# Block 0 of MLP1: tiles 4 to 15 in three passes of halves, and the three low bits of a decoded weight from ScalarE

## The chip, the cores and the metric

One core of a Trainium2 chip runs the whole program. The time is the device time of one execution in microseconds (us), the median of three runs. The profile is one further execution, with its own time. PE is TensorE's matmul stream, DVE is VectorE, ACT is ScalarE, SP is the engine that issues nearly all transfers.

## The reference, cut to what matters

```
kv  = einsum('bhsd,bhse->bhde', k, v);  out = einsum('bhsd,bhde->bhse', q, kv)   # 8 x 8 x 576 x 64
x   = out / sqrt(mean(out*out, -1) + 1e-6) * g_norm          # then as 4608 tokens x 512
h   = x @ w_in                                               # 512 -> 2048
g   = h * clip(h + 3, 0, 6) / 6
x1  = g @ w_out                                              # 2048 -> 512
out = (silu(x1 @ w_gate) * (x1 @ w_val)) @ w_out2            # 512 -> 1536 -> 512
```

`q`, `k`, `v` and `g_norm` come as 4-byte floats. The five weight matrices come as 8-byte floats, which no engine multiplies: the kernel reads each as two 4-byte words and puts a 4-byte float together from them.

## The kernel before, in words

The 4608 tokens are nine blocks of 512. Features lie on the partitions, tokens run along the free axis, so that `x` of a block is four tiles of 128x512 (`x_f[0][0..3]`), `h` is 16 tiles `h_0` to `h_15`, and `acc` four tiles in PSUM.

**Precision and what a product costs.** A plain 4-byte float product (`mm`, L116 to L118) is one MATMUL row in the program that PE works off at the float rate. The other form splits each operand into a high and a low half of the type fp32r, `split` (L106 to L109): ACT copies the tile to the high half (L108), DVE subtracts it from the tile for the low half (L109). The product is then three passes (`mm3`, L111 to L114): high times low, low times high, high times high.

**Decoding a weight.** `decode_w` (L154) makes a tile of 128x512 out of a raw tile of 128x4x128x2 words (512 KB). ACT scales the high word, read as a float (`decode_scale`, L167). Then DVE does three operations (`decode_bits`): a shift by three and a mask (L176, one tensor in and out), the sign by a bitwise or (L179), and the three low bits out of the raw tile's low word (L182). Raw tiles have three buffers, taken in turn by `raw_i` (w_in) and `raw_o` (w_out). The last reader of a raw tile is L182, and the load that takes its buffer next waits for that on SP's queue, L139 for w_in and L148 for w_out.

**Block 0** is where the weights of MLP1 are decoded. Its tiles are named by f: w_in tile f is `w_i{f}`, w_out tile f is `w_o{f}`. The loop starts behind the first stretch (whose order is written by hand, tiles 0 and 1 among it) and runs over c. In step c: `h_whole([c], 0)` makes `h_c` from `w_i{c}` with four plain products (L118); the attention for block 1 goes on, a third of a head pair per step (`kv` and `qT`, then `at` and `sq`, then `ss` and the norm L330 to L353); `o_first(c-2)` adds `g_{c-2}` times w_out to the four `acc` tiles in 12 passes (L112 to L114) and writes the halves of `w_o` to memory (`wod`); `get_o(c+1)` and `get_i(c+4)` decode and, for w_out, split (`wh_o`, `wl_o`); `raw_o(c+3)` and `raw_i(c+6)` load. Between `h` and `g` stand ACT's relu (L426), DVE's product (L427) and a split.

The four `split_x(1, ...)` and `split_wi` at the loop's end make the halves of block 1's x and of w_in tiles 0 to 3. From block 1 on, everything is made of halves: `split_wi` of tiles 4 to 7 stands in block 1's loop, and `make_wi` combines w_in tiles in pairs. The weights of MLP2 go through the same `decode_w` (24 tiles of gate and value, 12 of w_out2), most of them while the blocks of MLP1 and the first steps of MLP2 run.

**What sets the order.** PE's order is the order written in the program. In the block's loop the orders of ACT, DVE and SP come from the scheduler, which lays each engine's operations out by its own times; each engine then works its list off strictly in that order. So an operation that waits holds up all behind it on its engine.

Of the kernel before, what the change touches and what calls it, by code (L numbers as in the profile page):

```python
# [8 lines left out]
F32 = mybir.dt.float32  # L9
F32R = mybir.dt.float32r  # L10
U32 = mybir.dt.uint32
AF = mybir.ActivationFunctionType
ALU = mybir.AluOpType
AX = mybir.AxisListType
# [4 lines left out]
def kernel(  # L19
# [27 lines left out]
    nc = tc.nc  # L47
    P = 128
# [5 lines left out]
    KD = DM // P  # L54
    NF = DFF // P
    NF2 = DFF2 // P
    T = 512
    TQ = T // 2
# [12 lines left out]
    TO2 = TO // 2  # L71
    NP1 = NF // 2
    PWHOLE = 4

    def block_pieces(j):

# [47 lines left out]
    shift = const.tile([P, 1], F32, name="shift")  # L124
    gn38 = const.tile([P, 1], F32, name="gn38")
    three = const.tile([P, 1], F32, name="three")

    wod = dram.tile([NF, P, 2 * DM], F32, name="wod")
    x1d = dram.tile([P, KD, NT], F32, name="x1d")
# [23 lines left out]
    def w_slot(name, dtype):  # L153
        return wpool.tile([P, KD, P], dtype, tag="w", name=name)  # L154

    def decode_w(raw, name):

        return decode_bits(raw, decode_scale(raw, name))

    def decode_scale(raw, name):

        t = w_slot(f"w_{name}", F32)
        nc.scalar.activation(  # L167
            out=t, in_=raw[:, :, :, 1].bitcast(F32), func=AF.Copy, scale=2.0 ** -112
        )
        return t  # L170

    def decode_bits(raw, t):

        lw, hw = raw[:, :, :, 0], raw[:, :, :, 1]
        u = t.bitcast(U32)
        nc.vector.tensor_scalar(  # L176
            u, u, 3, 0x7FFFFFFF, op0=ALU.logical_shift_left, op1=ALU.bitwise_and
        )
        nc.vector.scalar_tensor_tensor(  # L179
            out=u, in0=hw, scalar=0x80000000, in1=u, op0=ALU.bitwise_and, op1=ALU.bitwise_or  # L180
        )
        nc.vector.scalar_tensor_tensor(  # L182
            out=u, in0=lw, scalar=29, in1=u, op0=ALU.logical_shift_right, op1=ALU.bitwise_or
        )
        return t
# [233 lines left out]
    def h_whole(cs, j):  # L419

        pss = {}
        for kk in range(KD):
            h_part(cs, j, kk, pss)
        for f, ps in pss.items():
            t = w_slot(f"t_{j}_{f}", F32).rearrange("p k f -> p (k f)")
            nc.scalar.activation(out=t, in_=ps, func=AF.Relu, bias=three[:, 0:1])  # L426
            nc.vector.scalar_tensor_tensor(  # L427
                out=t, in0=t, scalar=6.0, in1=ps, op0=ALU.min, op1=ALU.mult
            )
            split_g(j, f, t)  # L430

    whl, xhl = {}, {}

    def split_wi(f):
        whl[f] = split_w(wi[f], f"s{f}")

    def split_x(j, kk):

        if kk < 3:
            t = xpool.tile([P, 2, 2, TQ], F32R, tag=("B11", "B22", "B21")[kk], name=f"xs_{j}_{kk}")  # L440
            hi, lo = (t[:, i].rearrange("p k c -> p (k c)") for i in range(2))
        else:
            hi, lo = (w_slot(f"xs{o}_{j}_{kk}", F32R).rearrange("p k f -> p (k f)") for o in "hl")
        split(hi, lo, x_f[j][kk])
        xhl[kk] = hi, lo

    def h_part(cs, j, kk, pss):

        for f in cs:
            if kk == 0:  # L450
                pss[f] = pmm.tile([P, 512], F32, tag="mm", name=f"h_{j}_{f}")
            st, sp = kk == 0, kk == KD - 1
            if j:
                (wh, wl), (xh, xl) = whl[f], xhl[kk]
                mm3(pss[f], wh[:, kk], wl[:, kk], xh, xl, st, sp)
            else:
                mm(pss[f], wi[f][:, kk], x_f[j][kk], st, sp)
# [86 lines left out]
    def prepare_x1(j):  # L544

        x = x_f.pop(j)
        for key in XKEYS:
            if j == 1 and key[0] == "B":
                b = ("B11", "B12", "B21", "B22").index(key)
                xo1[key] = tuple(  # L550
                    [xhl[b // 2 * 2 + kk][i][:, b % 2 * TQ:(b % 2 + 1) * TQ] for kk in range(2)]
                    for i in range(2)
                )
                continue
            t = xpool.tile([P, 2, 2, TQ], F32R, tag=key, name=f"{key}_{j}")
            xo1[key] = t[:, 0], t[:, 1]

        def part(b, kk):

            c = slice(b % 2 * TQ, (b % 2 + 1) * TQ)  # L560
            if isinstance(x, list):
                return x[b // 2 * 2 + kk][:, c]
            return x[:, b // 2 * 2:b // 2 * 2 + 2, c]

        ts = {}
        for key, a, b in (("T1", 1, 0), ("T2", 3, "T1"), ("T3", 3, 1), ("T4", "T2", 2)):
            ts[key] = fpool.tile([P, 2, TQ], F32, tag="f", name=f"{key}_{j}")
            for kk in range(2) if isinstance(x, list) else (slice(None),):
                a_, b_ = (ts[o][:, kk] if isinstance(o, str) else part(o, kk) for o in (a, b))
                nc.vector.tensor_tensor(out=ts[key][:, kk], in0=a_, in1=b_, op=ALU.subtract)  # L570
        for key, b in (
            ("B11", 0), ("T1", None), ("T2", None), ("T3", None), ("B22", 3), ("B21", 2),
            ("T4", None),
        ):
            hi, lo = xo1[key]
            if isinstance(hi, list):
                continue
            if b is None:
                split(hi, lo, ts[key])
            else:  # L580
                for kk in range(2) if isinstance(x, list) else (slice(None),):
                    split(hi[:, kk], lo[:, kk], part(b, kk))
# [307 lines left out]
    with tc.manual_schedule(engines={mybir.EngineType.PE}):  # L890
# [3 lines left out]
            mybir.EngineType.Activation, mybir.EngineType.DVE, mybir.EngineType.SP,  # L894
        }))
        nc.vector.memset(eps, EPS)
        warm = const.tile([P, 1], F32, name="warm")
        for hp in range(NP):
            load_q(0, hp)
# [238 lines left out]
        for c in range(NF + LAG):  # L1138
            if c < NF:
                if c >= GROUP:  # L1140
                    h_whole([c], 0)
                for s, a in att_actions(1, (2, 5, 8, 11)):
                    if s == c:
                        a()
            if c >= LAG:
                o_first(c - LAG)
            if c >= NF + LAG - KD:
                split_x(1, c - NF - LAG + KD)
                split_wi(c - NF - LAG + KD)
            if c < NF:  # L1150
                get_o(c + 1)
                raw_o(c + 3)
                get_i(c + 4)
                raw_i(c + 6)
# [13 lines left out]
        for j in range(1, NB):  # L1168
            pairs = list(range(NP1))
            if j == 2:  # L1170
                pairs = pairs[PWHOLE:] + pairs[:PWHOLE]
            for i, p in enumerate(pairs):
                if j == 1 and p < PWHOLE:
                    hpair_whole(j, p)
                    if p == 0:
                        prepare_x1(j)
                else:
                    hpair(j, p)
                if j == 1 and i < 2:
                    for f in (2 * i + 4, 2 * i + 5):  # L1180
                        split_wi(f)
                if j == 1 and 2 <= i < 6:
                    make_wi(i + 2)
                if j == 2 and 1 <= i < 5:
                    make_wi(i - 1)
                for f in (2 * p, 2 * p + 1):
                    load_wo(f)
                if j + 1 < NB:
                    for s, a in att_actions(j + 1, (0, 1, 3, 4)):
                        if s == i:  # L1190
                            a()
                if i:
                    o_pair(j, pairs[i - 1], i == 1, False)
                if i == NP1 - 1:
                    if 1 < j + 1 < NB:
                        prepare_x1(j + 1)
                    o_pair(j, p, False, True)
                if j == NB - 1:
                    if i == NP1 - 2:
                        parts = prepare_x(0, x1, fpool)  # L1200
                        next(parts)
                    if i == 0:
                        ph1.__exit__(None, None, None)
                        big["xr"], raw2, big["x"] = (
                            mlp2.enter_context(tc.tile_pool(name=o, bufs=1, side="right"))
                            for o in ("xr", "raw2", "x1")
                        )
                        x1 = big["xr"].tile([P, KD, T2], F32, tag="xr", bufs=1, name="xr_0")
                    if 1 <= i <= KD:
                        nc.sync.dma_start(out=x1[:, i - 1], in_=x1d[:, i - 1, :T2])  # L1210
                    for _ in range(1 + (i % 2 and i < NP1 - 3)):
                        load_second()
            x1_out(j)
# [136 lines left out]
```

## Time and profile before

| | |
|---|---|
| three runs | 1677.17, 1678.15, 1678.41 us, median 1678.15 |
| the profiled execution | 1676.15 us, its span 1674.4 us |
| PE busy | 1655.1 us, 99% of the span |
| DVE busy | 1321.0 us, 79% |
| ACT busy | 809.4 us, 48% |
| PE's granted clock | 1.00 in each of 40 slices |

The span is the time between the first and the last event that the profile shows; 1.75 us of the execution lie around it. A busy share is a mean over stages with different limits. Block 0's loop lies between 35.59 us (the end of the first stretch) and 140.15 us (the end of `o_first(15)`). A wait is what ended the idle time of an engine.

### The profile page before, as it was taken

The page shows a single profiled execution, that of the slowest core. Times are in us where ns is not written, and L with a number is a line of the kernel's source. Part 1 is how long each engine was busy: PE and PEld are TensorE (multiplying, and loading weights), DVE is VectorE, ACT ScalarE, POOL GpSimd, SP SyncE. Part 2 cuts the span into 40 slices and gives each one's busy share as a digit, 9 for nine tenths or more (in the row PEclk, how much of TensorE's full clock was granted, in tenths as well). Part 3 has the DMA queues.
Part 4 walks back from the last instruction along what each step waited for, and adds up shares of the span by engine and source line. Part 5 has one row for each costly group of instructions (what it writes and reads, how often), then busy time and mean ns, then how long its engine had stood idle before and what let it go on. Part 6 is the DMA issues. An engine that isn't in the chain of part 4 may idle for free.

```text
span 1674.4 us, 27998 instructions
## 1 busy us (share of the span) xinstructions
PE 1655.1 (99%) x10640; PEld 1525.7 (91%) x10640; DVE 1321.0 (79%) x2535; ACT 809.4 (48%) x1489; POOL 2.4 (0%) x7
## 2 busy tenths in 40 slices
PE   7999999999999999999999999999999999999999
PEld 4567889899989899989889999999999999999999
DVE  6888997677787777677989988778998676887774
ACT  5655564544444454545565444444454444444432
POOL 0000000000000000000000000000000000000000
PEclk9999999999999999999999999999999999999999
DMA  8885445444535544325564544485453357655642
GB/s 233 260 260 177 135 146 145 146 133 146 148 113 157 142 141 130 126 98 185 170 202 166 195 161 146 175 275 191 164 190 144 138 208 272 214 194 196 217 159 97
DMA packets 224999, 288.63 MB, mean 172 GB/s; under 512 B 80992, under 2 KB 139360, under 8 KB 224864
## 3 DMA queue, kind: packets, MB, share of 16 engines
q1 hardware_dynamic: 220480, 285.80, 52.5%
q8 instruction: 83, 1.36, 0.3%
q10 hardware_dynamic: 4384, 1.05, 0.3%
q14 instruction: 52, 0.43, 0.1%
HBM read 211.03 MB, written 75.76 MB: 171 GB/s over the span
## 4 chain that ended last, share of the span: by engine, by line
PE 82%; DVE 10%; DMA 4%; ACT 3%; issue 1%; SPq 0%; DVEq 0%; ACTq 0%
PE q_g L588 15%; PE q_v L588 15%; PE a L588 7%; PE acc L112 6%; PE acc L113 6%; PE acc L114 6%; PE c L588 4%; PE o2c L836 4%; PE o2d L836 4%; PE o2a L836 4%; PE d L588 4%; PE o2e L836 2%; DVE g L109 1%; PE kv L271 1%; DMA raw_o<-in_moe_w_out_dram 1%
## 5 line engine op out<-in xcount | busy, mean ns | idle before, releaser
L112 PE MATMUL acc<-g,wo 128*128 128x512 f32 x512 | 202.3, 395 | 0.6 <-DVE g L109 0.6
L113 PE MATMUL acc<-g,wo 128*128 128x512 f32 x512 | 199.9, 390 | 0.0
L114 PE MATMUL acc<-g,wo 128*128 128x512 f32 x512 | 199.4, 390 | 0.0
L633 ACT ACTIVATE t<-h,three 128x512 f32<-128x512 f32 x120 | 86.9, 724 | 144.5 <-DVE h L630 113.1
L108 ACT ACTIVATE g<-t 128x512 fp32r<-128x512 f32 x142 | 89.5, 630 | 67.5 <-DVE t L634 55.6
L109 DVE TENSOR_TENSOR g<-t,g 128x512 fp32r<-128x512 f32 x142 | 96.6, 680 | 30.9 <-ACT g L108 30.3
L112 PEld LDWEIGHTS acc<-g,wo 128*128 128x128 f32 x512 | 96.2, 188 | 21.3 <-DVE g L109 1.5
L114 PEld LDWEIGHTS acc<-g,wo 128*128 128x128 f32 x512 | 96.1, 188 | 20.6
L113 PEld LDWEIGHTS acc<-g,wo 128*128 128x128 f32 x512 | 96.3, 188 | 18.3
L634 DVE SCALAR_TENSOR_TENSOR t<-t,h 128x512 f32<-128x512 f32 x120 | 82.4, 687 | 31.1 <-ACT t L633 29.7
L723 ACT ACTIVATE hg<-q_g 128x384 f32<-128x384 f32 x36 | 17.7, 491 | 117.5 <-PE q_g L588 117.5
L588 PE MATMUL q_v<-hT,v 128*128 128x384 f32 x288 | 73.6, 336 | 0.0
L730 DVE TENSOR_TENSOR hv<-hg,hv 128x1536 f32<-128x1536 f32 x36 | 63.1, 1753 | 5.1 <-ACT hv L723 4.9
L118 PE MATMUL h<-x,w_i 128*128 128x512 f32 x128 | 57.9, 595 | 2.3 <-DVE w_i L182 1.2
L723 ACT ACTIVATE hv<-q_v 128x384 f32<-128x384 f32 x36 | 17.7, 491 | 87.3 <-PE q_v L588 87.3
L712 DVE TENSOR_TENSOR h1v<-h1v,q_v 128x384 f32<-128x384 f32 x36 | 19.9, 553 | 48.3 <-ACT h1v L711 47.2
L588 PE MATMUL q_v<-hB,v 128*128 128x384 f32 x216 | 54.9, 335 | 0.0
L728 ACT ACTIVATE hg<-hg 128x1536 f32<-128x1536 f32 x36 | 53.6, 1490 | 0.9
L588 PE MATMUL a<-T,wh_i 128*128 128x256 f32 x240 | 53.2, 284 | 0.7 <-ACT s L607 0.5
L588 PE MATMUL c<-T,wh_i 128*128 128x256 f32 x240 | 53.0, 283 | 0.0
L588 PE MATMUL d<-T,wh_i 128*128 128x256 f32 x240 | 53.0, 283 | 0.0
L588 PEld LDWEIGHTS q_v<-hT,v 128*128 128x128 f32 x288 | 52.3, 188 | 0.0
(611 smaller groups left out, 5389.4 us busy)
## 6 DMA issues: line engine op xcount, KB each, us to landing
wo<-wod SPq DMA_DIRECT2D x128, 512.0 KB, 3.4
g2d<-hv SPq DMA_DIRECT2D x36, 768.0 KB, 3.7
graw<-g2d SPq DMA_DIRECT2D x26, 1024.0 KB, 7.2
xr<-x1d SPq DMA_DIRECT2D x10, 1536.0 KB, 7.0
gb<-g2d SPq DMA_DIRECT2D x54, 256.0 KB, 4.8
x1d<-x1o SPq DMA_DIRECT2D x36, 256.0 KB, 2.9
out_dram<-o SPq DMA_DIRECT2D x36, 256.0 KB, 2.5
raw_i<-in_moe_w_in_dram SPq DMA_DIRECT2D x16, 512.0 KB, 5.3
```

The lines of the kernel that those rows point to most:

```text
L108: nc.scalar.activation(out=hi, in_=src, func=AF.Copy)
L109: nc.vector.tensor_tensor(out=lo, in0=src, in1=f32(hi), op=ALU.subtract)
L112: nc.tensor.matmul(out_, wh, xl, start=start, stop=False)
L113: nc.tensor.matmul(out_, wl, xh, start=False, stop=False)
L114: nc.tensor.matmul(out_, wh, xh, start=False, stop=stop)
L118: nc.tensor.matmul(out_, f32(w), f32(x), start=start, stop=stop)
L588: nc.tensor.matmul(ps, a[:, kk], b[kk] if isinstance(b, list) else b[:, kk], start=first and n == 0, stop=n == 5, skip_group_check=True,)
L633: nc.scalar.activation(out=t, in_=h[i], func=AF.Relu, bias=three[:, 0:1])
L634: nc.vector.scalar_tensor_tensor(out=t, in0=t, scalar=6.0, in1=h[i], op0=ALU.min, op1=ALU.mult)
L728: nc.scalar.activation(out=hg, in_=hg, func=AF.Silu)
L730: nc.vector.tensor_tensor(out=hv, in0=hg, in1=hv, op=ALU.mult)
L836: nc.tensor.matmul(ps[:, i * TO2:(i + 1) * TO2], a[:, cs], b, start=first and i == 0 and n == 0, stop=n == 2, skip_group_check=True,)
```

## The change

Part one: block 0's tiles 4 to 15 are made of three passes of halves, as in later blocks. The halves of block 0's x (`split_x(0, kk)`, two calls each in steps 1 and 2) and of w_in tiles 4 to 15 (`split_wi(c + 2)`, one call a step) are made in the loop; those of tiles 4 to 7 are kept, so that block 1 need not make them again, those of tiles 8 to 15 are dropped. Part two: in `decode_w` ACT makes a second tile `y` out of the raw tile, the upper 16 bits of the low word times 2^-13 and less almost one half, rounded to an integer; DVE shifts the scaled tile by three and takes `y` in, in one operation (L171 of after), and then the sign (L174). The tiles of the first stretch (w_in 0 to 2, w_out 0) keep the old form.

```
-        return decode_bits(raw, decode_scale(raw, name))
+        t = decode_scale(raw, name)
+        y = w_slot(f"y_{name}", U32)
+        nc.scalar.activation(
+            out=y, in_=top16(raw), func=AF.Identity, scale=2.0 ** -13, bias=half[:, 0:1]
+        )
+        u = t.bitcast(U32)
+        nc.vector.scalar_tensor_tensor(
+            out=u, in0=u, scalar=3, in1=y, op0=ALU.logical_shift_left, op1=ALU.bitwise_or
+        )
+        nc.vector.scalar_tensor_tensor(
+            out=u, in0=raw[:, :, :, 1], scalar=0x80000000, in1=u,
+            op0=ALU.bitwise_and, op1=ALU.bitwise_or,
+        )
+        return t
+
+    def top16(raw):
+        r = raw.rearrange("p k f t -> p (k f t)").bitcast(U16)
+        return r.rearrange("p (k f t) -> p k f t", k=KD, t=4)[:, :, :, 1]
...
     def split_x(j, kk):
-        if kk < 3:
+        if j and kk < 3:
...
-            if j:
-                (wh, wl), (xh, xl) = whl[f], xhl[kk]
+            if j or f >= FWHOLE:
+                (wh, wl), (xh, xl) = whl[f], xhl[j, kk]
                 mm3(pss[f], wh[:, kk], wl[:, kk], xh, xl, st, sp)
             else:
                 mm(pss[f], wi[f][:, kk], x_f[j][kk], st, sp)
...
                 if c >= GROUP:
                     h_whole([c], 0)
+                    if c >= 2 * PWHOLE:
+                        whl.pop(c)
...
+            if 1 <= c <= 2:
+                for kk in (2 * c - 2, 2 * c - 1):
+                    split_x(0, kk)
+            if FWHOLE <= c + 2 < NF:
+                split_wi(c + 2)
...
-                if j == 1 and i < 2:
-                    for f in (2 * i + 4, 2 * i + 5):
-                        split_wi(f)
```

DVE, before, ahead of tile 4 and for the tiles around it: `w_i5` and `w_o3` are decoded, `t_0_2` and `g_0_2` are the gate of tile 2, `wl_o2` and `wl_o3` low halves of w_out.

```order
L109 TENSOR_TENSOR wl_o2_456<-w_o2_450,wh_o2_455 128x512
L176 TENSOR_SCALAR w_i5_461<-w_i5_461 128x512
L179 SCALAR_TENSOR_TENSOR w_i5_461<-raw_i5_423,w_i5_461 128x512
L427 SCALAR_TENSOR_TENSOR t_0_2_473<-t_0_2_473,h_0_2_468 128x512
L182 SCALAR_TENSOR_TENSOR w_i5_461<-raw_i5_423,w_i5_461 128x512
L176 TENSOR_SCALAR w_o3_536<-w_o3_536 128x512
L109 TENSOR_TENSOR g_0_2_476<-t_0_2_473,g_0_2_476 128x512
```

The same place on DVE, after: `wl_s4` is the low half of w_in tile 4, which `h_4` now needs, and `xsl_0_2` and `xsl_0_3` are low halves of block 0's x (those of 0 and 1 stand a few rows ahead).

```order
L111 TENSOR_TENSOR wl_o2_470<-w_o2_463,wh_o2_469 128x512
L171 SCALAR_TENSOR_TENSOR w_i5_475<-w_i5_475,y_i5_477 128x512
L448 SCALAR_TENSOR_TENSOR t_0_2_488<-t_0_2_488,h_0_2_483 128x512
L174 SCALAR_TENSOR_TENSOR w_i5_475<-raw_i5_425,w_i5_475 128x512
L111 TENSOR_TENSOR xsl_0_2_552<-x_0_2_347,xsh_0_2_551 128x512
L111 TENSOR_TENSOR g_0_2_491<-t_0_2_488,g_0_2_491 128x512
L111 TENSOR_TENSOR xsl_0_3_556<-x_0_3_349,xsh_0_3_555 128x512
L111 TENSOR_TENSOR wl_s4_560<-w_i4_447,wh_s4_559 128x512
L171 SCALAR_TENSOR_TENSOR w_o3_563<-w_o3_563,y_o3_565 128x512
```

What `h_4` waits for on DVE has moved from the decode of `w_i4`, ahead of these rows, to the eighth of them.

ACT, before, one step in the middle of the loop, from the split of `w_o6` to that of `w_o7` (`rs` and `nw` belong to the norm of block 1).

```order
L108 ACTIVATE wh_o6_729<-w_o6_724 128x512
L167 ACTIVATE w_i9_735<-raw_i9_604 128x512
L426 ACTIVATE t_0_6_747<-h_0_6_742,three_94 128x512
L167 ACTIVATE w_o7_776<-raw_o7_651 128x512
L108 ACTIVATE g_0_6_750<-t_0_6_747 128x512
L330 ACTIVATE rs_807<-ss_1_1_805,eps_91 128x512
L339 ACTIVATE nw_808<-rs_807 128x512
L344 ACTIVATE nw_808<-nw_808,shift_92 128x512
L108 ACTIVATE wh_o7_781<-w_o7_776 128x512
```

The same step on ACT, after.

```order
L110 ACTIVATE wh_o6_791<-w_o6_785 128x512
L188 ACTIVATE w_i9_797<-raw_i9_639 128x512
L167 ACTIVATE y_i9_799<-raw_i9_639,half_95 128x512
L447 ACTIVATE t_0_6_818<-h_0_6_805,three_94 128x512
L110 ACTIVATE wh_s8_847<-w_i8_701 128x512
L351 ACTIVATE rs_892<-ss_1_1_890,eps_91 128x512
L110 ACTIVATE g_0_6_821<-t_0_6_818 128x512
L188 ACTIVATE w_o7_851<-raw_o7_699 128x512
L167 ACTIVATE y_o7_853<-raw_o7_699,half_95 128x512
L360 ACTIVATE nw_893<-rs_892 128x512
L365 ACTIVATE nw_893<-nw_893,shift_92 128x512
L110 ACTIVATE wh_o7_857<-w_o7_851 128x512
```

Three operations have come in (`y_i9`, `wh_s8`, `y_o7`), and the scale of `w_o7` has moved behind `g_0_6`. PE's rows stay where they were; each of the tiles 4 to 15 has 12 rows for 4.

## Rows read from the trace of the kernel before

**Rows 1.** Windows (stretch, length, then busy time of each engine, granted clock, DMA).
```profile
35.59:64.25 28.66, 26.24 (x129) 16.82 (x129) 26.22 (x55) 17.11 (x35) 0.00 (x0) 1.00 0.73 225
64.25:85.93 21.68, 21.68 (x94) 13.56 (x93) 19.75 (x37) 13.19 (x24) 0.00 (x0) 1.00 0.87 284
...
800.00:1000.00 200.00, 198.17 (x1138) 188.73 (x1137) 180.00 (x345) 106.96 (x196) 0.00 (x0) 1.00 0.52 179
```
**Rows 2.** What PE waited for, 35.59 to 140.15 (total us, times, longest).
```profile
PE qT L289 <- DMA wod<-wl_o: 1.1, 1, 1.1
PE h L118 <- DVE t L427: 0.8, 1, 0.8
PE h L118 <- DVE w_i L182: 0.5, 1, 0.5
PE acc L112 <- DVE g L109: 0.3, 1, 0.3
```
**Rows 3.** PE's timeline (start, duration, group, in brackets the idle time before).
```profile
44.73 0.40 PE L112 MATMUL acc<-g,wh_o 128*128 128x512 f32 x1
...
47.47 3.60 PE L118 MATMUL h<-x,w_i 128*128 128x512 f32 x8
50.90 1.02 PE L118 MATMUL ss<-sq,ones 128*128 128x512 f32 x2
...
137.29 0.50 PE L112 MATMUL acc<-g,wh_o 128*128 128x512 f32 x1 [0.30 <-DVE g L109]
```
**Rows 4.** What ACT waited for most, 35.59 to 140.15.
```profile
ACT wh_o L108 <- DVE w_o L182: 19.0, 12, 2.8
```
**Rows 5.** DVE's timeline about tile 4, and the last gate.
```profile
44.57 0.69 DVE L182 SCALAR_TENSOR_TENSOR w_i<-raw_i,w_i 128x512 uint32<-128x512 uint32 x1
...
46.56 0.69 DVE L109 TENSOR_TENSOR wl_o<-w_o,wh_o 128x512 fp32r<-128x512 f32 x1 [0.70 <-ACT wh_o L108]
47.16 0.42 DVE L176 TENSOR_SCALAR w_i<-w_i 128x512 uint32<-128x512 uint32 x1
47.62 0.69 DVE L179 SCALAR_TENSOR_TENSOR w_i<-raw_i,w_i 128x512 uint32<-128x512 uint32 x1
48.34 0.69 DVE L427 SCALAR_TENSOR_TENSOR t<-t,h 128x512 f32<-128x512 f32 x1
...
136.55 0.68 DVE L109 TENSOR_TENSOR g<-t,g 128x512 fp32r<-128x512 f32 x1
```
**Rows 6.** ACT's timeline in the middle of the loop, and the last `wh_o`.
```profile
65.39 0.63 ACT L108 ACTIVATE wh_o<-w_o 128x512 fp32r<-128x512 f32 x1 [0.38 <-DVE w_o L182]
...
73.07 0.63 ACT L108 ACTIVATE wh_o<-w_o 128x512 fp32r<-128x512 f32 x1 [2.17 <-DVE w_o L182]
73.61 0.66 ACT L167 ACTIVATE w_i<-raw_i 128x512 f32<-128x512 f32 x1
74.17 0.66 ACT L426 ACTIVATE t<-h,three 128x512 f32<-128x512 f32 x1
...
78.86 0.72 ACT L344 ACTIVATE nw<-nw,shift 128x512 f32<-128x512 f32 x1 [0.87 <-DVE nw L340]
...
133.47 0.63 ACT L108 ACTIVATE wh_o<-w_o 128x512 fp32r<-128x512 f32 x1 [2.04 <-DVE w_o L182]
```
**Rows 7.** Loads of raw tiles, 35.59 to 140.15 (KB each, median us to landing).
```profile
raw_o<-in_moe_w_out_dram SPq DMA_DIRECT2D x13, 512.0 KB, 4.6
raw_i<-in_moe_w_in_dram SPq DMA_DIRECT2D x11, 512.0 KB, 5.2
```
**Rows 8.** SP's queue, its longest single wait in 35.59 to 140.15.
```profile
SPq L468 <- ACT wh_o L108: 8.0, 2, 5.2
```
**Rows 9.** PE at the start of the program: its longest wait, and two windows.
```profile
PE kv L271 <- DMA vA<-in_v_dram: 5.0, 1, 5.0
...
0.00:5.00 5.00, 0.00 (x0) 0.03 (x1) 1.66 (x8) 0.39 (x1) 2.44 (x7) 1.00 0.66 160
5.00:10.00 5.00, 2.75 (x25) 2.08 (x25) 1.04 (x3) 1.10 (x2) 0.00 (x0) 1.00 1.20 255
```

More of the change, by code (lines that the diff above doesn't have):

```diff
@@ L11 @@
 U32 = mybir.dt.uint32
+U16 = mybir.dt.uint16
 AF = mybir.ActivationFunctionType
@@ L73 @@
     PWHOLE = 4
+    FWHOLE = 4
     def block_pieces(j):
@@ L126 @@
     three = const.tile([P, 1], F32, name="three")
+    half = const.tile([P, 1], F32, name="half")
     wod = dram.tile([NF, P, 2 * DM], F32, name="wod")
@@ L444, in split_x @@
         split(hi, lo, x_f[j][kk])
-        xhl[kk] = hi, lo
+        xhl[j, kk] = hi, lo
     def h_part(cs, j, kk, pss):
@@ L550, in prepare_x1 @@
                 xo1[key] = tuple(
-                    [xhl[b // 2 * 2 + kk][i][:, b % 2 * TQ:(b % 2 + 1) * TQ] for kk in range(2)]
+                    [xhl[j, b // 2 * 2 + kk][i][:, b % 2 * TQ:(b % 2 + 1) * TQ] for kk in range(2)]
                     for i in range(2)
@@ L896 @@
         nc.vector.memset(eps, EPS)
+        nc.vector.memset(half, 2.0 ** -14 - 0.5)
         warm = const.tile([P, 1], F32, name="warm")
@@ L1149 @@
                 split_wi(c - NF - LAG + KD)
+            if 1 <= c <= 2:
[3 more added lines that the diff above has]
+                split_wi(c + 2)
+            if c == NF:
+                for kk in range(KD):
+                    xhl.pop((0, kk))
             if c < NF:
```

## The prediction

> **What bounds the kernel now.** I read the windows first. Over the whole span PE is busy 99%, so a change pays either by taking work off PE or by taking one of PE's few waits away, and it costs when it makes PE wait. From 800 to 1000 us PE loses under 2 us in 200 [rows 1]. In block 0's loop, where the change sits, PE runs without a gap from 64.25 to 85.93 us, three steps of the loop, while DVE is busy for 19.75 and ACT for 13.19 of these 21.68 us [rows 1]. PE's waits from 35.59 to 140.15 us add up to 2.7 us, of which the 0.5 for `w_i` comes before tile 4 [rows 2]. So PE is the bound, but DVE stands 2 us per three steps behind it, and DVE and ACT hand work to each other: ACT waits 19.0 us in twelve steps for the decoded `w_o` before it can split it [rows 4]. That idle time of ACT is no room for more work at any place: it lies between the last DVE step of a decode and ACT's copy, and in a queue worked off in order only what stands ahead of the copy can use it. The question is therefore whether the queue of ACT and DVE, with the new work in it, still keeps ahead of a PE that needs less.
>
> **What PE saves.** The plain tile 4 runs from 47.47 to 50.90, 3.43 us; the 12 passes of `o_first(1)` just ahead of it, of the same shapes, run from 44.73 to 47.47, 2.74 us [rows 3]. A tile in 12 passes saves 0.69 us, the twelve tiles 8.3 us. That is the most that part one can give, and three tiles are 2.07 us, so PE needs 21.68 - 2.07 = 19.6 us for three steps.
>
> **What DVE and ACT get.** On DVE an operation of two sources takes 0.68 us and the next starts 0.60 us after it, or 0.72 us if it needs its result (47.62 to 48.34 is that distance); the mask, one source, takes 0.42 [rows 5]. Each decode loses the 0.42 (0.33 of it in the queue, since ends overlap), and swaps one or for another. Each step gains one low half, 0.60. A step has two decodes: 0.60 - 0.66 is about nothing on DVE. ACT gains two `y` and one high half per step. A scale or a copy is followed by the next operation after 0.54 to 0.57 us (73.07, 73.61, 74.17) [rows 6].
>
> The operation `y` (16-bit words at a stride of 8 bytes, integers out, bias from a column) is in no row. The lower bound is the scale of the same raw tile, 0.66; the upper is the `nw` square, which also reads SBUF and takes a column as bias, 0.72 [rows 6]. I take 0.72, because the bias column is the feature that sets the two rows apart; the chain below is worked at 0.66 and corrected at its end. A gain below 0.66 has no row that speaks for it.
>
> That the mask is the cheap one of DVE's three operations speaks against the change: 0.42 against 0.69 for the sign [rows 5]. At the price of the two others DVE would lose 0.27 more per decode, 0.54 a step, and three steps would come out 1.6 us shorter where DVE ends the wait; by the row this is not had. The Trainium skill (VectorE: DVE Perf Modes, What auto-detection actually checks) gives the reason: an operation with a single source and its output in SBUF can use both read ports for it, one with two tensors can't in this type. The trace agrees with that rule, with 0.42 and 0.69.
>
> **The start of the loop.** Tile 4 stands at 47.47 without a wait, since `w_i4` was decoded from 44.57 on [rows 3, 5]. Now it needs the low half `wl_s4`, which is the seventh operation behind `wl_o2` on DVE. `wl_o2` starts at 46.56 [rows 5]; two low halves of x ahead of it (1.2) against the masks of three decodes (1.0) leave it about 0.2 later, at 46.8. Seven distances of 0.60 bring `wl_s4` to 51.0, its end to 51.7; with one more `y` that ACT must get through ahead of `wh_s4`, 0.57, the end is at 52.3. PE comes to tile 4 between 46.7 (no wait of 0.5 for `w_i` and no delay) and 47.5, and waits 5 to 6 us. This is paid once.
>
> **The pace after that.** I followed ACT's list from one `y_o` to the next. The leg over DVE is `y` 0.66, or 0.72, sign 0.72: 2.1 us until `wh_o` can start. A step without a norm or a `kv` then has eight operations of ACT (`wh_o`, `w_i`, `y_i`, relu, `wh_s`, `rs`, `g`, `w_o`) of 0.52 to 0.57, 4.4 us: together 6.5. In the step with the norm's second part the leg is 2.6 (DVE's `nw` stands between or and sign) and ACT has 5.1, 7.7. In the step with the next head pair's `at` it is 2.1, 4.3 and 0.8 of waiting for PE's `at`, 7.2 to 7.3. Three steps are 21.5 us, where PE had 21.68 and would now need 19.6. So after the start ACT and DVE set the pace, at almost the pace of before, and PE waits some 2 us in three steps, mostly at `h` for `wl_s` and at `qT` for the norm's x. The 0.69 per tile goes there.
>
> Followed through, `wh_o5` starts at 68.3 for 65.39, and `y_o6` at 72.8, so `wh_o6` at 74.9 for 73.07 [rows 6]; `wh_o15` at 135.9 for 133.47 [rows 6], the gate's low half `g_15` at 139.0 for 136.55 [rows 5], and `o_first(15)` at 139.7 for 137.29 [rows 3]. The delay of 2 to 3 us is the one from the start, carried along. Block 0 ends 2.4 us later. With 0.72 for `y`, two of them a step on this path and 14 steps, 14 x 2 x 0.05 = 1.4 us more: 3.8.
>
> **Raw tiles.** Buffers go free at the sign now, the second of DVE's two operations, and `y` reads the raw tile too. In my chain a load is issued 6.75 to 9.15 us ahead of the scale that needs it, and lands after 4.6 or 5.2 us [rows 7]. I cost this at nothing; what hides it is the 1.5 us between 5.2 and 6.75.
>
> **Later.** Block 1 no longer splits tiles 4 to 7: four operations of ACT and four of DVE less, where PE loses little; I take -0.7 us, between 0 and -1. The 36 decodes of MLP2 lose 0.33 on DVE and gain 0.6 on ACT each; where PE loses under 1% of the time [rows 1] that is 0, with 1 to 2 us to either side.
>
> **The sum.** On the profiled execution, 1676.15: + 3.8 - 0.7 = 1679.2. That execution lies 2.0 under the median of 1678.15, so the median comes to about 1681.
>
> **Rivals.** *PE stays the bound* after the start: then the wait of 4.8 us at tile 4 (52.3 for 47.47) is followed by the rest of the loop, 92.7 us, less the waits of 2.2 and less 8.3: block 0 ends 5.7 us earlier, 1672.4 on the median. For it speaks ACT's 19.0 us of idle time [rows 4]; against it, that this idle time is the DVE leg, which stays. It is decided by a step of ACT and DVE of under 6.5 us. *The pace is a little better* (three steps in 20.6 us, as when a scheduler's order lets ACT fill part of the leg): 3 to 4 us of gain over the loop, 1677.5, no change.
>
> *Raw tiles late*, the case on the slow side if the pace is right: DMA is at 0.87 from 64 to 86 us already [rows 1], SP's queue holds loads behind stores that wait for `wh_o`, once for 5.2 us [rows 8], and `wh_o` is now later. If landing takes over 6.75 us from the issue it costs its excess in each step; 0.5 us in ten steps are 5 us, 1686.
>
> *The clock falls at the new wait.* The rows show a granted clock of 1.00 in the windows before and after PE's 5.0 us wait at the program's start, and no wait over 1.1 us after 35.59 [rows 2, 9]; so a wait of 5.8 us amid work has no row here. If the clock went down to 1.2 GHz for the 12 passes of tile 4, their 2.74 us would be 5.5: +2.7, 1683.7. The Trainium skill (TensorE: Matmul & The Clock Gate, Part 1: The HAM clock gate) says that the clock is halved after an idle time of PE; that no row at the lower level stands in this trace leaves it open.
>
> **How the numbers follow.** Forecast 0.50, PE stays the bound 0.22, a little better pace 0.10, raw tiles late 0.12, clock 0.06. A measurement of this kernel can tell about 0.2% from no change, 3.4 us, so "the same" is 1674.8 to 1681.5. The forecast, 1681 with 2 us to either side for `y`, block 1 and MLP2, lies across its upper end: 0.30 same, 0.18 slower, 0.02 faster. The second rival adds 0.10 to same, the first 0.22 to faster, the last two 0.18 to slower: faster 0.24, same 0.40, slower 0.36. The range goes from 1672, which takes in the first rival, to 1687, past raw tiles late.
>
> **What would show it.** Right: one wait of PE of 5 to 6 us at the first `h` in passes, ended by `wl_s` on DVE, and some 2 us per three steps after it, at `h` and `qT`; twelve passes of `h` in 2.74 us; `y` at 0.72; `o_first(15)` at 139 to 142 us; nothing but 1 us to either side after block 0. Wrong: PE without waits from 60 us on and block 0 ending at 134 us (the queue's pace was taken too long); ACT's scale waiting for raw tiles in most steps (the loads); a `y` of 0.8 us or more; a granted clock under 1.00 about 52 us; a gain or a loss of several us after 200 us.

## The result

| | before | after |
|---|---|---|
| median of four runs | 1678.21 us | 1689.26 us (1687.62 to 1690.46) |
| ratio | | 1.0063, 95% interval 1.0050 to 1.0075 |
| profiled execution, its span | 1674.4 us | 1687.4 us |
| end of `o_first(15)` | 140.15 us | 149.92 us |
| DVE busy, ACT busy | 1321.0, 809.4 us | 1308.6, 856.0 us |

The kernel became 11 us slower. The forecast was 1681 with a range to 1687, so the direction was among its cases and the size was not. Of the 13.0 us between the two spans, 9.8 lie in block 0. PE's last pass of MLP1's `acc` stands 10.5 us later (874.5 for 864.0), so block 1 gave nothing back, and the other 2.5 came in MLP2. The profiled execution of before lies 2.1 us under its median and that of after on its median, which is why the spans differ by more than the medians do (11.1); in which stage these 2 us lie isn't shown.

The windows of after (stretch, length, busy times of PE, PE's weight loads, DVE, ACT and POOL, granted clock, DMA share, GB/s), the first two over the stretches of [rows 1], the third the three steps from `h_9` to `h_12`:

```profile
35.59:64.25 28.66, 23.57 (x104) 16.35 (x104) 23.68 (x46) 22.92 (x46) 0.00 (x0) 0.88 0.71 215
64.25:85.93 21.68, 20.91 (x124) 16.18 (x124) 18.88 (x32) 17.53 (x34) 0.00 (x0) 1.00 0.86 258
...
90.29:112.98 22.69, 20.21 (x105) 15.61 (x105) 18.79 (x32) 17.79 (x33) 0.00 (x0) 1.00 0.76 222
...
800.00:1000.00 200.00, 198.09 (x1143) 187.94 (x1142) 176.02 (x334) 118.14 (x214) 0.00 (x0) 1.00 0.54 187
```

In the first stretch PE is busy for 23.57 us where it was 26.24, and the mean clock is 0.88. Three steps take 22.69 us where they took 21.68 and 21.67: PE idles, although neither ACT (17.79) nor DVE (18.79) is full. From 800 to 1000 us PE is as busy as before (198.09 and 198.17).

What PE waited for in after, 30 to 165 us (total, times, longest); it answers [rows 2]:

```profile
PE h L114 <- ACT wh_s L110: 5.0, 2, 4.6
PE qT L310 <- issue: 3.1, 2, 1.6
PE h L115 <- DVE wl_s L111: 2.9, 4, 0.9
PE acc L114 <- DVE g L111: 2.4, 2, 2.2
PE qT L310 <- DVE x L374: 0.4, 1, 0.4
```

PE's timeline in after, about tile 4 and at `o_first(15)`; the first row is the last pass of `o_first(1)`:

```profile
47.09 0.39 PE L116 MATMUL acc<-g,wh_o 128*128 128x512 f32 x1
52.07 0.80 PE L114 MATMUL h<-xsl,wh_s 128*128 128x512 f32 x1 [4.58 <-ACT wh_s L110]
53.37 0.80 PE L115 MATMUL h<-xsh,wl_s 128*128 128x512 f32 x1 [0.51 <-DVE wl_s L111]
53.97 0.63 PE L116 MATMUL h<-xsh,wh_s 128*128 128x512 f32 x1
54.39 0.63 PE L114 MATMUL h<-xsl,wh_s 128*128 128x512 f32 x1
...
57.71 1.02 PE L120 MATMUL ss<-sq,ones 128*128 128x512 f32 x2
...
145.47 0.51 PE L114 MATMUL acc<-g,wh_o 128*128 128x512 f32 x1 [2.17 <-DVE g L111]
145.81 0.60 PE L115 MATMUL acc<-g,wl_o 128*128 128x512 f32 x1
146.21 0.63 PE L116 MATMUL acc<-g,wh_o 128*128 128x512 f32 x1
```

and the windows of the granted clock there (same columns):

```profile
48.00:50.00 2.00, 0.00 (x0) 0.00 (x0) 1.50 (x3) 2.00 (x4) 0.00 (x0) 1.00 0.78 237
50.00:52.00 2.00, 0.00 (x0) 0.00 (x0) 2.00 (x4) 1.74 (x5) 0.00 (x0) 0.56 0.88 261
52.00:54.00 2.00, 1.42 (x3) 0.82 (x4) 1.97 (x5) 1.22 (x3) 0.00 (x0) 0.50 0.86 129
...
56.00:58.00 2.00, 2.00 (x7) 1.48 (x7) 1.47 (x4) 1.65 (x3) 0.00 (x0) 0.73 1.00 341
...
144.00:146.00 2.00, 0.53 (x2) 0.49 (x3) 2.00 (x5) 1.46 (x3) 0.00 (x0) 0.96 0.62 162
146.00:148.00 2.00, 2.00 (x6) 1.52 (x6) 0.62 (x2) 0.60 (x1) 0.00 (x0) 0.50 0.00 0
```

PE stood for 4.6 us at tile 4, until ACT had made `wh_s4`, and after the first pass for 0.5 more, until DVE had made `wl_s4`; 5 to 6 were forecast. The clock fell to its lower level (0.50, 1.2 GHz) while it stood, so tile 4 took from 52.07 to 57.71, and a pass followed the last after 0.43 us in place of 0.23. At `o_first(15)` the clock fell after a wait of 2.2 us: its 12 passes took 4.45 us (145.47 to 149.92).

ACT and then DVE of after, about the step in which a head pair ends and the next begins. The `y_o` are those of tiles 6, 7, 8 and 9, the `wh_o` those of 7 and 8:

```profile
75.33 0.77 ACT L167 ACTIVATE y_o<-raw_o,half 128x512 uint32<-128x512 uint16 x1
...
82.05 0.77 ACT L167 ACTIVATE y_o<-raw_o,half 128x512 uint32<-128x512 uint16 x1
...
84.81 0.61 ACT L110 ACTIVATE wh_o<-w_o 128x512 fp32r<-128x512 f32 x1
...
90.61 0.73 ACT L167 ACTIVATE y_o<-raw_o,half 128x512 uint32<-128x512 uint16 x1
93.67 0.63 ACT L110 ACTIVATE wh_o<-w_o 128x512 fp32r<-128x512 f32 x1 [2.32 <-DVE w_o L174]
...
98.04 0.76 ACT L167 ACTIVATE y_o<-raw_o,half 128x512 uint32<-128x512 uint16 x1
```
```profile
90.18 0.69 DVE L111 TENSOR_TENSOR g<-t,g 128x512 fp32r<-128x512 f32 x1 [0.64 <-ACT g L110]
90.88 0.23 DVE L111 TENSOR_TENSOR kvbd<-kv,kvbd 64x64 fp32r<-64x64 f32 x1
91.14 0.69 DVE L111 TENSOR_TENSOR qlo<-qT,qhi 128x512 fp32r<-128x512 f32 x1
91.75 0.68 DVE L171 SCALAR_TENSOR_TENSOR w_o<-w_o,y_o 128x512 uint32<-128x512 uint32 x1
92.35 0.69 DVE L111 TENSOR_TENSOR xs<-x,xs 128x512 fp32r<-128x512 f32 x1
92.95 0.68 DVE L174 SCALAR_TENSOR_TENSOR w_o<-raw_o,w_o 128x512 uint32<-128x512 uint32 x1
94.33 0.69 DVE L111 TENSOR_TENSOR wl_o<-w_o,wh_o 128x512 fp32r<-128x512 f32 x1 [0.70 <-ACT wh_o L110]
```

The leg from `y_o` to `wh_o` takes 3.06 us here: DVE comes to `w_o` 1.14 us after `y_o` has started (0.41 after its end), because `g`, `kvbd` and `qlo` stand ahead in its list, and `xs` lies between its two operations. In that time ACT waits for 2.32 us, and then DVE waits for ACT.

### The profile page after: what moved, and what is told of

Its sections match the earlier page's. It is cut to its first block, busy times and chain, and to the rows that moved or that the text cites. A ratio compares the mean times of both kernels' runs of the same rounds, so it can differ in the third digit from the quotient of the medians.

```text
span 1687.4 us, 28126 instructions
## 1 busy us (share of the span) xinstructions
PE 1654.8 (98%) x10688; PEld 1537.3 (91%) x10688; DVE 1308.6 (78%) x2484; ACT 856.0 (51%) x1565; POOL 2.4 (0%) x7
## 4 chain that ended last, share of the span: by engine, by line
PE 81%; DVE 9%; ACT 4%; DMA 3%; issue 2%; SPq 0%; DVEq 0%; ACTq 0%
PE q_g L609 14%; PE q_v L609 14%; PE acc L114 7%; PE a L609 7%; PE acc L115 6%; PE acc L116 6%; PE c L609 4%; PE d L609 4%; PE o2c L857 3%; PE o2d L857 3%; PE o2a L857 3%; PE o2e L857 2%; PE kv L292 1%; PE h L115 1%; DMA graw<-g2d 1%
## 5 line engine op out<-in xcount | busy, mean ns | idle before, releaser
L744 ACT ACTIVATE hg<-q_g 128x384 f32<-128x384 f32 x36 | 17.7, 492 | 105.2 <-PE q_g L609 105.2
L744 ACT ACTIVATE hv<-q_v 128x384 f32<-128x384 f32 x36 | 17.7, 492 | 80.0 <-PE q_v L609 80.0
L110 ACT ACTIVATE gxh<-gt 128x1024 fp32r<-128x1024 f32 x26 | 27.4, 1056 | 50.0 <-DVE gt L785 50.0
L110 ACT ACTIVATE gyh<-gb 128x512 fp32r<-128x512 f32 x54 | 32.2, 623 | 39.9 <-DMA gb<-g2d 39.7
```

The source lines that it names most:

```text
L110: nc.scalar.activation(out=hi, in_=src, func=AF.Copy)
L744: nc.scalar.activation(out=h[:, 0], in_=a, func=AF.Copy)
```

## The experiments

Theory A was the forecast's own: ACT and DVE hand work to each other in lists worked off in order, and this sets the pace of the loop. The rivals were: one of the two parts alone is to blame (B), the clock (C), the wait at the start (D). The runs were made in three groups, each on one chip with its own runs of the kernel before: e1 to e4 (1678.20 us), e5 to e8 (1677.94), e9 and e10 (1678.07).

### The parts alone

Part one alone, `decode_w` as before:

```
-        t = decode_scale(raw, name)
-        y = w_slot(f"y_{name}", U32)
...
+        return decode_bits(raw, decode_scale(raw, name))
```

> Part one alone: tiles 4 to 15 in passes, decode as in the kernel before (three operations of DVE, no y). Theory A (the queue of ACT and DVE sets the pace of the loop, and both parts load it): ACT has 1.3 us less per step than in the changed kernel, DVE 0.66 more; three steps come to 21.5 to 22.3 us, the wait at tile 4 stays at 4 to 5 us: 1680 to 1685 us. Theory B (the longer decode by way of ACT is the cause, the passes are a gain): PE is the bound after the start, 1671 to 1675 us.

Measured: 1685.15 us, ratio 1.0046 (1.0031 to 1.0061). PE's wait at tile 4 is 4.5 us here too, block 0 ends at 147.4, and three steps (`h_6` to `h_9`, `h_9` to `h_12`) take 21.0 and 21.7 us. B falls for the passes: they lose on their own. A holds here, just past the slow end of what it said (1685).

Part two alone:

```
-    FWHOLE = 4
+    FWHOLE = NF
...
-            if FWHOLE <= c + 2 < NF:
-                split_wi(c + 2)
...
+                if j == 1 and i < 2:
+                    for f in (2 * i + 4, 2 * i + 5):
+                        split_wi(f)
```

> Part two alone: y on ACT in every decode, all tiles of block 0 in plain products. Theory A: without wh_s and wl_s ACT and DVE need 20.5 to 21.3 us for three steps, PE 21.68, so PE stays the bound and the time is that of the kernel before, 1677 to 1680 us. Theory B: the slow decode delays wh_o and wl_o in every step, 1683 us or more. For later stages: whatever lies over 1679 after block 0 is the price of y in MLP2 (0 to 2 us).

Measured: 1676.33 us, ratio 0.9988 (0.9979 to 0.9998), a hair faster than A said. What PE waited for from 35.59 to 149 us, all of it:

```profile
PE qT L310 <- DVE t L448: 1.2, 1, 1.2
PE h L120 <- DVE t L448: 0.5, 1, 0.5
```

Block 0 ends at 138.6. So the two parts are +6.9 and -1.9 us, and together +11.1: the decode by way of ACT saves 1.9 with all tiles in plain products, where PE hardly waits, and costs 4.1 on top of the passes. The parts don't add up; that the bound changes between them is the reading which the runs of the late split, below, test.

### The clock

```
             st, sp = kk == 0, kk == KD - 1
+            if j == 0 and f == FWHOLE and st:
+                for q4 in range(KD):
+                    mm(pss[f], wi[f][:, q4], x_f[j][q4], q4 == 0, q4 == KD - 1)
```

> The changed kernel, but tile 4 is made twice: first in four plain products, which PE can do while it waits for wl_s4, then in the 12 passes over it, from zero. PE's wait falls from 4.6 us to about 1. Theory C (the fall of the clock at this wait is what the forecast missed): granted clock 1.00 about 52 us, tile 4's passes 2.74 us in place of 5.6, block 0 ends 2.5 to 3 us earlier and the time is 1686 to 1687 us. Theory A: ACT and DVE are late anyway; only the 1.1 us that ACT waited for PE's ss comes back, 1688 to 1689 us.

PE's timeline and windows of this kernel at the same two places:

```profile
46.83 3.60 PE L120 MATMUL h<-x,w_i 128*128 128x512 f32 x8
51.61 0.51 PE L114 MATMUL h<-xsl,wh_s 128*128 128x512 f32 x1 [1.18 <-ACT wh_s L110]
52.92 0.50 PE L115 MATMUL h<-xsh,wl_s 128*128 128x512 f32 x1 [0.81 <-DVE wl_s L111]
...
145.39 0.50 PE L114 MATMUL acc<-g,wh_o 128*128 128x512 f32 x1 [2.22 <-DVE g L111]
145.73 0.40 PE L115 MATMUL acc<-g,wl_o 128*128 128x512 f32 x1
```
```profile
52.00:54.00 2.00, 1.20 (x6) 0.91 (x6) 1.97 (x4) 0.78 (x2) 0.00 (x0) 1.00 0.66 207
...
146.00:148.00 2.00, 2.00 (x10) 1.66 (x9) 1.24 (x2) 0.78 (x2) 0.00 (x0) 1.00 0.06 23
```

The clock stays at 1.00 at tile 4, but the time doesn't move: 1689.71 us, ratio 1.0075 (1.0060 to 1.0090), a little above what A said. The profiled execution took 1688.02 us, the fastest of the four; the other three show a mean clock of 0.998 or 0.999, so it fell somewhere in them. `wh_o5` starts at 70.9, in after at 70.8, and `h_9` at 90.3 in both: what PE wins at tile 4 it waits for behind ACT and DVE. So C falls for the start. At `o_first(15)` the clock fell in after's profile, behind a wait of 2.17 us, and didn't in this one, behind 2.22; block 0 ends 1.7 us earlier by that. In the medians of the two it can't be seen.

### The handing over

`w_o f` is split one step later than it is decoded, the rest as in the changed kernel:

```
         def get_o(f):
-            if f < NF:
-                wo[f] = split_w(decode_w(raws.pop(("o", f)), f"o{f}"), f"o{f}")
+            if f - 1 in dec_o_late:
+                wo[f - 1] = split_w(dec_o_late.pop(f - 1), f"o{f - 1}")
+            if f < NF:
+                dec_o_late[f] = decode_w(raws.pop(("o", f)), f"o{f}")
```

> The changed kernel, but the split of w_o f into halves is written one step later than its decode (o_first needs it two steps later still), so that ACT does not stand waiting for DVE's decode. Theory A: ACT's waits at wh_o (16.7 us in eleven steps) shrink to under 4, three steps take 20 to 21 us in place of 22.8, block 0 ends 6 to 9 us earlier: 1680 to 1683 us. If the pace is set by something else (transfers, DVE's own work of 18 to 19 us in three steps), no change within 1.5 us: 1688 to 1690.

Measured: 1679.48 us, ratio 1.0008 (0.9999 to 1.0018): 9.8 us under the changed kernel, with the same operations, and a little better than A said. What ACT waited for most in block 0's loop, first in this kernel, then in after:

```profile
ACT g L110 <- DVE t L448: 3.9, 10, 0.9
ACT sq L333 <- PE at L116: 3.0, 3, 2.4
ACT w_i L188 <- DMA raw_i<-in_moe_w_in_dram: 2.8, 3, 1.6
```
```profile
ACT wh_o L110 <- DVE w_o L174: 16.7, 11, 2.3
ACT x1o L517 <- PE acc L116: 3.4, 2, 2.0
```

The wait at `wh_o` is gone, three steps (`h_9` to `h_12`) take 20.2 us, and block 0 ends at 138.1. A holds. The scheduler laid out all lists anew, so the wait at tile 4 shrank as well (0.98 and 0.80 us for 4.58 and 0.51); but tile 4 starts only 0.6 us earlier (51.5 for 52.1), and of the 11.8 us by which block 0 ends earlier, most come after it.

The control is the same edit in the kernel before:

> The kernel before with the late split of w_o alone, a control: here PE is the bound and ACT's wait of 19.0 us costs nothing, so theory A expects no change: 1677 to 1679 us. A gain of 3 us or more would say that the late split pays by itself, and that its effect on the changed kernel is no sign of what bounds that.

Measured: 1676.71 us, ratio 0.9993 (0.9984 to 1.0003), no change. The 19.0 us of waiting in the kernel before [rows 4] cost nothing; the 16.7 us of the changed kernel cost it its gain.

### The start

The late split, and passes from tile 6 on, the halves of block 0's x one step later, so that tiles 4 and 5 need no halves:

```
-    FWHOLE = 4
+    FWHOLE = 6
...
-            if 1 <= c <= 2:
-                for kk in (2 * c - 2, 2 * c - 1):
+            if 2 <= c <= 3:
+                for kk in (2 * c - 4, 2 * c - 3):
```

> The changed kernel with the late split of w_o, the passes only from tile 6 on (tiles 4 and 5 in plain products) and the halves of x one step later, so that no wait stands at tile 4. Theory A (queue of ACT and DVE, now without its standing wait, keeps ahead of PE): ten tiles save 6.9 us on PE, the start loses nothing: block 0 ends at 132 to 134 us for 140.2, and the time is 1670 to 1673 us. If ACT and DVE still set the pace once PE is on time (their 6.4 us a step against PE's 6.5), half of it: 1674 to 1676.

Measured: 1677.89 us, ratio 1.0003 (0.9993 to 1.0012), above both of the ranges set down. Three steps take 19.6 us (`h_9` at 88.2, `h_12` at 107.8), what PE needs; but between 60 and 71 us PE waited 1.6, 2.25 and 0.9 us. PE's timeline, and ACT's, of this kernel there, and a window of the granted clock behind it:

```profile
68.85 0.47 PE L114 MATMUL at<-qlo,kvbd 128*128 128x448 f32 x1 [2.25 <-ACT kvbd L110]
70.21 0.47 PE L115 MATMUL at<-qhi,kvbd 128*128 128x448 f32 x1 [0.89 <-DVE kvbd L111]
```
```profile
66.68 0.66 ACT L188 ACTIVATE w_i<-raw_i 128x512 f32<-128x512 f32 x1 [2.18 <-DMA raw_i<-in_moe_w_in_dram]
...
68.57 0.22 ACT L110 ACTIVATE kvbd<-kv 64x64 fp32r<-64x64 f32 x1
```
```profile
72.00:74.00 2.00, 2.00 (x7) 1.51 (x6) 1.26 (x3) 2.00 (x5) 0.00 (x0) 0.50 0.86 243
```

A raw tile landed late, ACT stood for 2.2 us, and behind it `kvbd`, on which PE waited; then the clock fell, and the passes of `o_first` came 0.43 us apart. The raw tiles late, a rival of the forecast, are real in every kernel with the late split: ACT's waits for `raw_i` in block 0 add up to 1.7 to 17.7 us in these six, 4.7 here and 17.7 in the control, where the kernel before has 1.4 and the changed kernel none. The late split takes ACT's wait for DVE away and brings in part a wait for the loads.

The same without the late split, and so the changed kernel without its wait at the start:

> As the run before, but the split of w_o where the changed kernel has it (ACT waits for DVE's decode in each step). Theory A: the pace of 22.8 us for three steps stays and is the loss; the wait at tile 4 is gone, but ACT and DVE are little earlier: 1685 to 1688 us. Theory D (the loss is the wait at the start, with the clock's fall behind it): the 5 us come back and the passes gain, 1678 us or less.

Measured: 1684.05 us, ratio 1.0038 (1.0024 to 1.0053). The wait at tile 4 is gone, and yet the window from `h_9` to `h_12` reads:

```profile
88.10:110.80 22.70, 20.17 (x105) 15.59 (x104) 18.81 (x32) 17.83 (x33) 0.00 (x0) 1.00 0.74 221
```

22.7 us, as in after, and the same operations with the late split took 19.6 and 6.2 us less in all. Without its wait at tile 4 the changed kernel gives back 5 us, and still loses 6; D is a part, not the cause.

The late split and the passes from tile 6, with the decode of the kernel before:

> As the first of these runs, but every weight decoded as in the kernel before (no y, three operations of DVE). Theory A: ACT is free for it (1.3 us less a step), DVE has 0.66 more a step, some 6.6 to 6.7 us of its own work per step against PE's 6.5; DVE then sets the pace and most of the gain goes: 1673 to 1677 us, 2 to 4 above the first run. If y costs more on ACT than it saves on DVE even here: below the first run.

Measured: 1681.70 us, ratio 1.0023 (1.0013 to 1.0033), 3.8 above the same with `y`, as A said, though both lie higher than it said. With the late split the decode by way of ACT is a gain of 3.8 us, without it a loss of 4.1. How much of the 3.8 is the decode's own work isn't shown: ACT waited for raw tiles for 12.9 us here and for 4.7 in the kernel with `y`.

### A version that is faster than both

```
-    FWHOLE = 4
+    FWHOLE = 8
...
-            if 1 <= c <= 2:
-                for kk in (2 * c - 2, 2 * c - 1):
-                    split_x(0, kk)
+            if 3 <= c <= 6:
+                split_x(0, c - 3)
```

with the late split, and block 1's splits of tiles 4 to 7 put back.

> The late split of w_o, passes only from tile 8 on, the four halves of block 0's x spread over steps 3 to 6, block 1's four splits of w_in tiles where the kernel before has them. Eight tiles save 5.5 us on PE. In the run with passes from tile 6 a raw tile of w_in came 2.2 us late at 66 us, behind a DVE that had worked without a pause for 12 us, and PE lost 5 us there. Theory A: with that crowding spread out the queue keeps ahead of PE all along, block 0 ends at 133 to 135 us and the time is 1671 to 1675. If the crowding comes from the loop's own work at the pair boundaries, PE loses 3 to 5 us again: 1676 to 1679.

Measured: 1675.26 us, ratio 0.9980 (0.9972 to 0.9989). The time lies just over what A said (1671 to 1675). Block 0 ends at 133.5, as A said, 6.6 us earlier than before; PE waited 2.5 us from 35.59 to 149, and the clock stayed at 1.00 in the loop. From `h_9` to `h_12`:

```profile
84.10:103.80 19.70, 19.60 (x106) 15.78 (x105) 18.39 (x32) 18.13 (x33) 0.00 (x0) 1.00 0.77 228
```

Beside after's 22.69, with 18.79 us of DVE and 17.79 of ACT, this is the same work in 3.0 us less. Of the 6.6 us, 2.8 show in the medians. In the profiled execution PE's last pass of `acc` is 4.9 us earlier (859.1), the last output tile 0.3 (1670.9 for 1671.2): 4.6 are lost in MLP2, where PE waited 2.3 us for ACT in the last stage and the clock read 0.50 behind it (1474 to 1476 us). The two profiled executions lie differently to their medians, before's 2 us under its own, so the 0.3 understates the gain.

The same in plain products, to see what the late split does without the passes:

> Part two alone with the late split of w_o: all tiles of block 0 plain, y on ACT. Theory A: PE is the bound in the loop with 21.7 us for three steps, so this is part two alone again, 1675 to 1678 us; only small waits at the start can differ.

Measured: 1676.57 us, ratio 0.9988 (0.9979 to 0.9997), the same as part two alone. So of the 2.8 us, 1.5 come without any passes. The other 1.3, between these two kernels, are hardly clear of the noise: the eleven times of each overlap (1673.04 to 1678.65 and 1674.99 to 1678.07).

## Why the prediction was wrong

**What held.** PE needs 0.69 us less per tile (12 passes in 2.74 us where the clock is full). The wait at tile 4: 4.6 us and 0.5 more, `wl_s4` done at 53.3 for a forecast 52.3. ACT and DVE set the pace afterwards, through ACT's wait for the decode of `w_o`: the late split, its control and the run from tile 6 show it. Raw tiles were in time in the changed kernel (no wait of ACT for them among its waits). PE's remaining waits were at `h`, `qT` and `acc`.

**The step that failed is the size of what ACT and DVE cost PE: the delay out of the start, and the pace after it.** `wh_o` came 2.5 us late against the chain that was worked out at `w_o5` (70.8 for 68.3), 2.7 at `w_o6` and 5.7 at `w_o15` (141.65 for 135.9).

The first 2.5 us stand there before the pace can count: the delay that the start leaves, against the kernel before, is 5.4 us at `w_o5` for a forecast of 2.9. Of the 2.5, 1.0 is there at `wl_s4`, and 0.5 is the leg from `y_o5` to `wh_o5` (2.62 us for 2.1); the rest isn't traced.

The pace is the other part. Forecast: three steps 21.5 us at 0.66 for `y`, 21.8 at 0.72. Measured: 22.7, as 6.72, 8.56 and 7.43 from `y_o6` to `y_o9` for 6.5, 7.7 and 7.2 to 7.3. Two terms were too small. The `y` took 0.75 us (0.73 to 0.77), above both bounds, and the next operation of ACT followed after 0.65: 0.08 more than in the chain, six times in three steps, 0.5 us. (The forecast's own correction for 0.72 was a little short too: two operations a step by 0.06 over 14 steps are 1.7 us, not 1.4.) And in the step with the norm's second part I set ACT's part at 5.1 us; measured are 5.80 from `wh_o7` to `y_o8` (84.81 to 90.61). In the step after it the leg over DVE took 3.06 us for 2.1: I had counted what DVE does for `w_o` and not what stands ahead of it in DVE's list at that moment. This was luckily made up, since the 0.8 of waiting for PE's `at` that I had put into the same step did not come (4.37 us from `wh_o8` to `y_o9` for 5.1).

**The end was worse.** From `wh_o15` to the end of block 0 before took 6.7 us and after 8.3. The difference is the clock behind the wait for `g_15`, in the profiled execution: the 12 passes took 4.45 us there for 2.86 in before. The clock was named as a rival at the first wait only. It fell there, by the size given (tile 4 in 5.6 us), and the filler shows that it cost nothing there, since ACT and DVE were late anyway. The Trainium skill (TensorE: Matmul & The Clock Gate, Part 1: The HAM clock gate) has the clock halved after an idle time of PE; the trace agrees, with 0.50. The chance of 0.06 rested in part on a wrong reading of [rows 9]. The clock column says 1.00 there, but in the trace of the kernel before the same two products take 2.08 us some 5 us after that first wait and 1.02 later, so the lower level does stand in it:

```profile
9.90 2.08 PE L118 MATMUL at<-qhi,kv 128*128 128x512 f32 x2 [1.15 <-DVE kv L990]
...
15.37 1.02 PE L118 MATMUL at<-qhi,kv 128*128 128x512 f32 x2
```

**Block 1 and later.** The -0.7 us for block 1 did not come: 9.8 us at the end of block 0 and 10.5 at PE's last pass of `acc`. MLP2 was 0 with 1 to 2 us to either side; in the profiles its last stage took 2.0 us longer than before. Part one alone, whose lists of ACT are the same as before's in that stage, has 1.8 us of it too, with PE waiting for ACT's copies there, and that wait differs from one execution to the next (0 to 2.3 us). But from PE's last pass of `acc` to the last output tile the kernel before took 807.2 us and the control with the late split 806.9, and all ten kernels with either part of the change 808.6 to 811.8 (after 809.8). So the change seems to have a part in it; by what way stays open.

**The rivals.** "PE stays the bound" was wrong for the change and became true with the late split and passes from tile 6 or 8 on: 19.6 to 19.7 us for three steps, as worked out (19.6). Its 0.22 was too much for the change as written; the slower side deserved more than 0.36.

## What to carry to other kernels

Where two engines hand work back and forth in fixed lists, busy shares don't tell the pace: 18 and 19 us of work took 22.7 us, and with the consumer's operation moved one step later in the list the same work took 19.6 (the two runs from tile 6). So before giving such a pair more work, put a step between producer and consumer, and only then count what each engine has; the same operation moved to the other engine cost 4.1 us with the wait in place and saved 3.8 with the late split. When a chain is followed by hand, count what stands ahead of each step in its engine's list, and not the step's own operations alone.

## What the runs showed of the hardware

- The granted clock of after fell to 0.50 while PE stood for 4.6 us, and read 0.50 from 52 to 56 us. Behind a wait of 2.17 us it fell in after, and behind one of 2.22 us in another kernel's profile at the same place it did not. In the run with the late split it stood at a mean of 0.66 from 45 to 50 us, behind a stretch from 40 to 45 in which PE was busy for 3.55 us and waited 1.45 in one piece; the passes of `o_first(1)` came 0.43 us apart there. Of the eight profiled kernels with passes in block 0, all but the filler's and the last version's show such a fall in block 0; of the four with plain products alone, none.
- An ACT operation that reads 16-bit words at a stride of 8 bytes from SBUF, with a column as bias, and writes 4-byte integers took 0.75 us for 128x512, the scale of the same raw tile 0.66. The Trainium skill (ScalarE: Activation LUTs, What ACT_TABLE_LOAD costs) gives 280 ns + 0.833 ns per element for such a bias, an estimate of 0.71; the trace doesn't agree, and its 0.75 decides.
